# The last group of a fused filter-and-MLP kernel: turned by TensorE, stored in two transfers, with the bound on |h| behind the first layer

## The chip, the cores and the metric

One Trainium2 chip, one of its cores. The metric is the device time of one launch in microseconds; the time before is the median of three runs. A profile is one execution; its span is a few microseconds shorter than the launch.

## What is computed

```python
X = np.fft.rfft(x, axis=1)                    # x: 8 x 3008 x 256
Y = X * (filt_r + 1j * filt_i)[None, :, :]
y = np.fft.irfft(Y, n=3008, axis=1).astype(np.float32)
t = y.reshape(8 * 3008, 256)                  # 24064 tokens
h = t @ w_in                                  # w_in: 256 x 2048
g = h - np.tanh(h)
out = (g @ w_out).astype(np.float32)          # w_out: 2048 x 256
```

The transforms are factored as 64 x 47 and done as products. The second part, two layers around `h - tanh(h)`, is most of the work.

## The kernel before

The tokens are cut into 48 groups of up to 512 columns, over five units of one or two batch entries. A group goes through four steps `u` of the hidden layer. Each layer is done as seven products of half-size blocks instead of eight, with sums of blocks on both sides (q = 1 to 7). The main loop is a pipeline over `U = 4 * group + u`: `up(U)` is the first layer, `shrink(U - 1)` the function, `down(U - 2)` the second layer. All three are woven together by the hooks `d, e` (next piece of `down`), `s` (next piece of `shrink`) and `t(k)` (stores, transforms of the next unit, other side work). The order written is the order on each engine. Line numbers such as L622, used below and in the profile, are given as comments.

The function, and the block sums that follow it on GpSimd:

```python
def combine(b, t):
    G.tensor_sub(t[0], b[0][1], b[0][0])        # L462
    G.tensor_sub(t[1], b[1][1], t[0])           # L463
    G.tensor_sub(t[2], b[1][1], b[0][1])        # L464
    G.tensor_sub(t[3], t[1], b[1][0])           # L465
```

```python
# up(U), first layer                             # products: L483
mm(X, 1, True); mm(Y, 2, True); s1 = copied("s1")     # copies on ScalarE: L489
t(0); d(); s()
V.tensor_add(h[:, 0, :, 0:w], Y, s1)            # L499
e(); s(); s(); t(1)
mm(X, 6, False); mm(Z, 5, True); u2 = copied("u2")
d(); s(); e(); t(2)
mm(X, 7, False); u3 = copied("u3")
V.tensor_add(h[:, 3, :, 0:w], Z, u3)            # L513
d(); s(); e(); t(3)
mm(X, 4, False)
V.tensor_copy(h[:, 2, :, 0:w], X)               # L519
s(); d(); e(); t(4)
mm(Z, 3, False)
V.tensor_add(h[:, 1, :, 0:w], Z, u2)            # L525
```

`shrink` has six pieces: for k = 2 and then 0, `start(k)` (ScalarE, L539 and L540: y), `square(k)` (VectorE L544: h*y; ScalarE L545), `end(k)` (VectorE L548), and behind the last one `combine`.

The second layer adds into four PSUM banks over the four steps. In the last step the blocks of the output are put together:

```python
mm(1, 2)                                        # products: L590
yield
if done:                                        # done = (u == 3)
    ACT.copy(p1, product(1))                    # L603
    V.tensor_add(o[:, 0, 0:w], product(2), p1)  # L604
yield
mm(3, 5)
yield
if done:
    ACT.copy(p5, product(5))                    # L609
    V.tensor_add(x12, product(3), p5)           # L610
yield
mm(6, 7)
yield
if done:
    V.tensor_add(u2, product(6), p1)            # L615
    V.tensor_add(p1, product(7), u2)            # L616
yield
mm(4)
yield
if done:
    V.tensor_add(o[:, 1, 0:w], product(4), p1)  # L621
    G.tensor_add(o[:, 0, w:2 * w], u2, x12)     # L622
    G.tensor_add(o[:, 1, w:2 * w], p1, p5)      # L623
    accs.pop(i)
    stores.append((i, o))
yield
```

`o` has the features in the partitions and the tokens along the rows; the output in memory is the other way round. `store`, called at `t(2)` of the next step, turns it in blocks of 32 x 32 and prepares 32 transfers with rows of 32 floats; four of them are issued at every `t(k)`:

```python
def store(i, o):
    ot = dn.tile([128, 2, CH * 128], F32, tag="ot", bufs=1, name="ot")
    for h in range(2):
        V.transpose(ot[:, h, 0:total], o[:, h, 0:total])     # L637
    # ... blocks: four quarters of the partitions, with their first rows in memory
    for h in range(2):
        for k in range(4):
            for row, m, lo in blocks:
                outs.append((dram(...), ot[32 * k:32 * k + 32, h, :]...))

def store_some(n):
    for dst, src in outs[:n]:
        nc.sync.dma_start(dst, src)                          # L655
    del outs[:n]
```

The function is done by a form that holds for small |h| alone. `bounded` multiplies |w_in| with the largest |t| of each group, which bounds |h|, and counts whether all lie below `NEAR`; behind everything each engine loads the count, and only if it isn't full is the general path run (it isn't run with these inputs).

```python
def bounded(z):
    # ...
    for half in range(2):
        pb = z("pb", [128, NP, ng])                          # ng = 48 groups
        for t in range(NP):                                  # NP = 8
            w_abs = tr.tile([128, 2, 128], F32, tag="x", bufs=3, name="w_abs")
            cols = slice(t * 128, (t + 1) * 128)
            if half == 0:
                ACT.activation(w_abs, wu[:, 0:2, cols], AF.Abs)                 # L671
            else:
                V.tensor_add(w_abs[:, 0], wu[:, 4, cols], wu[:, 3, cols])       # L673
                ACT.activation(w_abs[:, 0], w_abs[:, 0], AF.Abs)                # L674
                ACT.activation(w_abs[:, 1], wu[:, 3, cols], AF.Abs)             # L675
            for h in range(2):
                nc.tensor.matmul(pb[:, t], w_abs[:, h], largest[:, h], ...)     # L677
        V.tensor_single_scalar(out=small[:, half], in_=pb, scalar=NEAR, op=ALU.is_lt)  # L679
        yield
    V.tensor_reduce(out=least, in_=small, axis=mybir.AxisListType.XYZ, op=ALU.min)     # L682
    nc.tensor.matmul(pc, least, ones, start=True, stop=True)                    # L684
    V.tensor_copy(count, pc)                                                    # L685
    yield
```

It is called in `t(k)` of the main loop, three times in the first step of the last group:

```python
if i == len(groups) - 1 and k in (0, 2, 4):
    next(bounds, None)
```

and the end of the kernel is

```python
for w in stores:
    store(*w)
store_some(len(outs))
# ...
within = nc.values_load(count[0:1, 0:1], min_val=0, max_val=128)    # L1060, on every engine
with tc.If(within < 128):                                           # L1061
    ...
```

Of the kernel before, what the change touches and what calls it, by code (L numbers as in the profile page):

```python
# [66 lines left out]
def _consts():  # L67
    wq = np.exp(-2j * np.pi * np.outer(np.arange(NQ), np.arange(NQ)) / NQ)
    wr = np.exp(-2j * np.pi * np.outer(np.arange(NR), np.arange(NR)) / NR)
    tw = np.exp(-2j * np.pi * np.outer(np.arange(NQ), np.arange(NR)) / SEQ)  # L70


    f1 = np.zeros((NQ, 64))
    f1[:, 0:31] = wq.real[:, 1:32]
    f1[:, 31] = wq.real[:, 0]
    f1[:, 32:63] = wq.imag[:, 1:32]
    f1[:, 63] = wq.real[:, 32]

    wf1 = np.zeros((2, 128, 64, 2))
    for b in range(2):  # L80
        wf1[0, 64 * b:64 * b + 64, :, b] = f1
        wf1[1].reshape(128, 2, 64)[64 * b:64 * b + 64, b] = f1
    wf1 = wf1.reshape(2, 128, 128).transpose(1, 0, 2)

    perm = np.arange(NR)
    perm[LO:] = LO + NR - 1 - perm[LO:]
    f2 = np.zeros((NK, R2, R2))
    for a in range(31):  # L90
        wp = (wr * tw[a + 1][None, :])[perm, :]
        f2[a, 0::2] = np.concatenate([wp.real.T, wp.imag.T], axis=1)
        f2[a, 1::2] = np.concatenate([-wp.imag.T, wp.real.T], axis=1)
    f2[:, :, NR + LO:] *= -1.0
    w0, w32 = wr * tw[0][None, :], wr * tw[32][None, :]
    f2[31, 0::2, 0:LO] = w0.real.T[:, 0:LO]
    f2[31, 0::2, NR + 1:NR + LO] = w0.imag.T[:, 1:LO]
    f2[31, 1::2, LO:NR] = w32.real.T[:, 0:HI]
    f2[31, 1::2, NR + LO:R2] = w32.imag.T[:, 0:HI]
    f2[31, 1::2, NR] = w32.real.T[:, HI]  # L100


    f2w = np.zeros((NK, R2, 128))
    f2w[:, :, 0:NR], f2w[:, :, IM:IM + NR] = f2[:, :, :NR], f2[:, :, NR:]


    ctw = np.exp(2j * np.pi * np.outer(np.arange(33), np.arange(NR)) / SEQ)
    g = np.zeros((NK, IM + NR, R2))
    for a in range(31):
        t1 = (wr.conj() * ctw[a + 1][:, None]) / SEQ  # L110
        tr, ti = t1.real.T[perm, :], t1.imag.T[perm, :]
        g[a, :NR, :NR], g[a, :NR, NR:] = tr, ti
        g[a, IM:, :NR], g[a, IM:, NR:] = -ti, tr
    g[:, IM + LO:] *= -1.0
    t0 = (wr.conj() * ctw[0][:, None] / SEQ).T
    t32 = (wr.conj() * ctw[32][:, None] / SEQ).T
    g[31, 0, :NR] = t0.real[0]
    g[31, IM, NR:] = t32.real[HI]
    g[31, 1:LO, :NR], g[31, IM + 1:IM + LO, :NR] = 2 * t0.real[1:LO], -2 * t0.imag[1:LO]
    g[31, LO:NR, NR:], g[31, IM + LO:, NR:] = 2 * t32.real[0:HI], -2 * t32.imag[0:HI]  # L120


    w = np.exp(2j * np.pi * np.outer(np.arange(NQ), np.arange(33)) / NQ)
    s = np.zeros((64, NQ))
    s[0:62:2] = 2.0 * w.real[:, 1:32].T
    s[1:62:2] = -2.0 * w.imag[:, 1:32].T
    s[62] = w.real[:, 0]
    s[63] = w.real[:, 32]
    s2 = np.zeros((128, 128))
    for b in range(2):  # L130
        s2[64 * b:64 * b + 64, 64 * b:64 * b + 64] = s


    fg = np.zeros((IM + RP, NK, 128 + RP2))
    fg[:R2, :, :128] = f2w.transpose(1, 0, 2)
    fg[:IM + NR, :, 128:].reshape(IM + NR, NK, 2, RP)[..., :NR] = \
        g.transpose(1, 0, 2).reshape(IM + NR, NK, 2, NR)

    return [np.ascontiguousarray(v, dtype=np.float32) for v in (wf1, fg.reshape(IM + RP, -1), s2)]


@with_exitstack
def kernel(
# [8 lines left out]
):  # L152
    nc = tc.nc
    V, G, ACT = nc.vector, nc.gpsimd, nc.scalar
    wf1_d, fg_d, s2_d = (
        nc.inline_tensor(v, name=n).ap() for v, n in zip(_consts(), ("wf1", "fg", "s2")))


    ct1 = [nc.dram_tensor(f"ct1_{p}", (RP, 64 * len(bs), DM), F32, kind="Internal")
# [298 lines left out]
        uts[i] = (b, tu, w)  # L458
        yield

    def combine(b, t):
        G.tensor_sub(t[0], b[0][1], b[0][0])  # L462
        G.tensor_sub(t[1], b[1][1], t[0])  # L463
        G.tensor_sub(t[2], b[1][1], b[0][1])  # L464
        G.tensor_sub(t[3], t[1], b[1][0])  # L465


# [59 lines left out]
    def shrink(U):  # L527

        h, w = hs.pop(U)
        ht = {k: h[:, k:k + 2].rearrange("p a b n -> p (a b) n")[:, :, 0:w] for k in (0, 2)}  # L530

        def tiles(tag, bufs):
            return dn.tile([128, 4, 256], F32, tag=tag, bufs=bufs, name=tag)[:, :, 0:w]

        y, sq = {}, {}

        def start(k):
            y[k] = tiles("y", 2)
            ACT.activation(y[k], ht[k], AF.Arctan, scale=S)  # L539
            ACT.activation(y[k], y[k], AF.Square)  # L540

        def square(k):
            sq[k] = tiles("sq", 1)
            V.tensor_mul(ht[k], ht[k], y[k])  # L544
            ACT.activation(sq[k], y[k], AF.Square, bias=near_b, scale=A)  # L545

        def end(k):
            V.scalar_tensor_tensor(out=ht[k], in0=sq[k], scalar=K, in1=ht[k],  # L548
                                   op0=ALU.add, op1=ALU.mult)

        start(2)
        yield
        square(2)
        yield
        end(2)
        yield
        start(0)
        yield
        square(0)
        yield  # L560
        end(0)
        t = dn.tile([128, 4, 2, 256], F32, tag="t", bufs=2, name="t")
        blocks = [[h[:, 2 * a + k, :, 0:w] for k in range(2)] for a in range(2)]
        combine(blocks, [t[:, k, :, 0:w] for k in range(4)])
        gs[U] = (blocks, t, w)
        yield

# [2 lines left out]
    def down(U):  # L570
# [12 lines left out]
        def product(q):  # L583
            bank, k = at[q]
            return acc[bank][:, k, 0:w]
# [28 lines left out]
        if done:  # L614
            V.tensor_add(u2, product(6), p1)  # L615
            V.tensor_add(p1, product(7), u2)  # L616
        yield
        mm(4)
        yield
        if done:  # L620
            V.tensor_add(o[:, 1, 0:w], product(4), p1)  # L621
            G.tensor_add(o[:, 0, w:2 * w], u2, x12)  # L622
            G.tensor_add(o[:, 1, w:2 * w], p1, p5)  # L623
            accs.pop(i)
            stores.append((i, o))
        yield

    def store(i, o):
# [15 lines left out]
# [3 lines that stand above are left out]
# [3 lines left out]
                        ot[32 * k:32 * k + 32, h, :].rearrange(  # L650
                            "p (j c) -> p j c", c=128)[:, 0:m, lo:lo + 32]))

    def store_some(n):
        for dst, src in outs[:n]:
            nc.sync.dma_start(dst, src)  # L655
        del outs[:n]

    def bounded(z):


        ng = len(groups)
        small = tr.tile([128, 2, NP, ng], F32, tag="a2", bufs=2, name="small")
        ones = cst.tile([128, 1], F32, name="ones")
        G.memset(ones, 1.0)
        for half in range(2):
            pb = z("pb", [128, NP, ng])
            for t in range(NP):
                w_abs = tr.tile([128, 2, 128], F32, tag="x", bufs=3, name="w_abs")
                cols = slice(t * 128, (t + 1) * 128)
                if half == 0:  # L670
                    ACT.activation(w_abs, wu[:, 0:2, cols], AF.Abs)  # L671
                else:
                    V.tensor_add(w_abs[:, 0], wu[:, 4, cols], wu[:, 3, cols])  # L673
                    ACT.activation(w_abs[:, 0], w_abs[:, 0], AF.Abs)  # L674
                    ACT.activation(w_abs[:, 1], wu[:, 3, cols], AF.Abs)  # L675
                for h in range(2):
                    nc.tensor.matmul(pb[:, t], w_abs[:, h], largest[:, h],  # L677
                                     start=(h == 0), stop=(h == 1), skip_group_check=True)
            V.tensor_single_scalar(out=small[:, half], in_=pb, scalar=NEAR, op=ALU.is_lt)  # L679
            yield  # L680
        least = cst.tile([128, 1], F32, name="least")
        V.tensor_reduce(out=least, in_=small, axis=mybir.AxisListType.XYZ, op=ALU.min)  # L682
        pc = z("pc", [1, 1])
# [3 lines that stand above are left out]
# [69 lines left out]
    with tc.tile_pool(name="tr", bufs=2) as tr:  # L756
# [184 lines left out]
        with tc.tile_pool(name="dn", bufs=2) as dn, \  # L941
                tc.tile_pool(name="ps", bufs=1, space=bass.MemoryType.PSUM) as ps:

            psums.append(lambda name, shape: ps.tile(shape, F32, tag="t", bufs=1, name=name))

            def tiles1(k, dtype, n):

                tag = {"raw": "ft", "it": "uv", "pt": "zs", "st": "e1", "ft": "a2"}[k]
# [24 lines left out]
            with tc.manual_schedule():  # L973
# [3 lines left out]
                for U in range(total + 2):  # L977
# [39 lines left out]
                    def t(k):  # L1017
# [11 lines left out]
                        elif done < len(steps) and steps[done] <= pos:  # L1029
# [5 lines left out]
                            if done == n_f:  # L1035
                                ms = middle(p + 1, z1)
                                next(ms)
                        if i == len(groups) - 1 and k in (0, 2, 4):
                            next(bounds, None)
                        if k in (0, 2, 4):  # L1040
                            next(late, None)
                        elif U > 0:
# [2 lines left out]
                    if U < total:  # L1045
                        if i == len(groups) - 1 and u == 0:
                            bounds = bounded(z1)
                        up(U, d, e, s, t)
                    else:
                        for k in range(5):  # L1050
# [2 lines left out]
                            d()  # L1053
                            e()
                            t(k)
                for w in stores:
                    store(*w)
                store_some(len(outs))
# [36 lines left out]
```

## Time and profile before

| | before |
|---|---|
| time, median of 3 (lowest to highest) | 2882.33 us (2880.47 to 2883.72) |
| span of the profiled run | 2879.3 us |
| busy: TensorE products, VectorE, ScalarE, GpSimd | 95%, 69%, 65%, 61% |
| mean granted clock of TensorE | 0.984 |
| transfers of L655 | 1536 |
| products of the bound, L677 | 64 instructions, from 2787.1 to 2799.9 us |
| last output turned (L637); last transfer issued | 2858.2 us; 2873.8 us |

PE is TensorE, PEld its loads of weights, DVE is VectorE, ACT ScalarE, POOL GpSimd, SP SyncE. A q behind the name means the engine's sequencer or its queue. A product of fp32 operands is shown as two instructions. In a line on waits, the numbers are microseconds in total, how often, and the longest. Matmul ends are modelled, so idle time of PE in such lines is a lower limit.

### The profile page before, as it was taken

The page shows a single profiled execution, that of the slowest core. Times are in us where ns is not written, and L with a number is a line of the kernel's source. Part 1 is how long each engine was busy: PE and PEld are TensorE (multiplying, and loading weights), DVE is VectorE, ACT ScalarE, POOL GpSimd, SP SyncE. Part 2 cuts the span into 40 slices and gives each one's busy share as a digit, 9 for nine tenths or more (in the row PEclk, how much of TensorE's full clock was granted, in tenths as well). Part 3 has the DMA queues.
Part 4 walks back from the last instruction along what each step waited for, and adds up shares of the span by engine and source line. Part 5 has one row for each costly group of instructions (what it writes and reads, how often), then busy time and mean ns, then how long its engine had stood idle before and what let it go on. Part 6 is the DMA issues. An engine that isn't in the chain of part 4 may idle for free.

```text
span 2879.3 us, 36469 instructions
## 1 busy us (share of the span) xinstructions
PE 2748.1 (95%) x12474; PEld 2278.9 (79%) x12474; DVE 1989.3 (69%) x2214; ACT 1872.2 (65%) x2460; POOL 1743.4 (61%) x1382
## 2 busy tenths in 40 slices
PE   5789999999999999999999999999999999999996
PEld 3467777888878787888877888888888888888885
DVE  4675666766776677766677777766777777777765
ACT  3555666666767676666666676666666676666663
POOL 4345777544677767645576777655476666555544
PEclk7889999999999999999999999999999999999998
DMA  9644443232233332222323233112233222110100
GB/s 270 180 150 116 114 110 91 62 93 81 70 76 84 76 75 53 57 81 83 87 71 75 68 78 81 36 45 67 51 75 81 53 55 56 24 28 16 26 11 16
DMA packets 328061, 217.46 MB, mean 76 GB/s; under 512 B 229085, under 2 KB 280405, under 8 KB 327674
## 3 DMA queue, kind: packets, MB, share of 16 engines
q1 hardware_dynamic: 273176, 160.50, 23.6%
q10 hardware_dynamic: 52738, 51.33, 5.9%
q0 software_dynamic: 1952, 3.22, 0.5%
q8 instruction: 100, 1.64, 0.2%
q14 instruction: 95, 0.78, 0.1%
HBM read 138.81 MB, written 79.17 MB: 76 GB/s over the span
## 4 chain that ended last, share of the span: by engine, by line
PE 69%; DVE 9%; ACT 8%; POOL 5%; issue 4%; DMA 3%; SPq 1%; ACTq 0%; DVEq 0%; POOLq 0%
PE o L590 27%; PE x L483 18%; PE z L483 8%; PE y L483 5%; PE pe L364 3%; PE pu L447 3%; DVE h L544 3%; PE pz L383 3%; ACT y L539 2%; PE pf L304 2%; ACT y L540 1%; POOL t L465 1%; ACT u L489 1%; DVE uv L398 1%; DVE h L519 1%
## 5 line engine op out<-in xcount | busy, mean ns | idle before, releaser
L590 PE MATMUL o<-t,wd 128*128 128x256 f32 (+2 forms) x3072 | 777.9, 376 | 1.8 <-POOL t L464 1.3
L544 DVE TENSOR_TENSOR h<-h,y 128x1024 f32<-128x1024 f32 (+2 forms) x384 | 589.7, 1536 | 256.1 <-ACT y L540 255.9
L462 POOL TENSOR_TENSOR t<-h 128x512 f32<-128x512 f32 (+2 forms) x192 | 240.1, 1250 | 767.5 <-DVE h L548 582.3
L590 PEld LDWEIGHTS o<-t,wd 128*128 128x128 f32 x3072 | 582.0, 191 | 74.4 <-POOL t L464 1.9
L483 PE MATMUL x<-tu,wu 128*128 128x256 f32 (+2 forms) x2304 | 592.2, 380 | 16.5 <-ACT u L489 15.5
L590 PE MATMUL o<-h,wd 128*128 128x256 f32 (+2 forms) x2304 | 581.6, 375 | 0.2 <-DVE h L548 0.2
L548 DVE SCALAR_TENSOR_TENSOR h<-sq,h 128x1024 f32<-128x1024 f32 (+2 forms) x384 | 566.6, 1476 | 20.8 <-ACT y L539 0.5
L483 PEld LDWEIGHTS x<-tu,wu 128*128 128x128 f32 x2304 | 430.2, 191 | 157.2 <-issue 73.2
L590 PEld LDWEIGHTS o<-h,wd 128*128 128x128 f32 x2304 | 431.3, 190 | 70.8 <-issue 18.5
L545 ACT ACTIVATE sq<-y,near_b 128x1024 f32<-128x1024 f32 (+2 forms) x384 | 435.4, 1134 | 5.8 <-DVE h L548 1.1
L539 ACT ACTIVATE y<-h 128x1024 f32<-128x1024 f32 (+2 forms) x384 | 400.0, 1042 | 14.8 <-ACT e L367 6.8
L489 ACT COPY s<-x 128x512 f32<-128x512 f32 (+2 forms) x192 | 110.7, 577 | 458.2 <-PE x L483 449.6
L540 ACT ACTIVATE y<-y 128x1024 f32<-128x1024 f32 (+2 forms) x384 | 399.3, 1040 | 12.2
L465 POOL TENSOR_TENSOR t<-t,h 128x512 f32<-128x512 f32 (+2 forms) x192 | 306.7, 1597 | 0.0
L489 ACT COPY u<-x 128x512 f32<-128x512 f32 (+2 forms) x384 | 219.2, 571 | 73.0 <-PE x L483 35.5
L399 POOL TENSOR_TENSOR zs<-zs,ft 128x512 f32<-128x512 f32 x112 | 166.3, 1485 | 142.3 <-ACT zs L397 142.2
L463 POOL TENSOR_TENSOR t<-h,t 128x512 f32<-128x512 f32 (+2 forms) x192 | 241.6, 1258 | 15.0
L464 POOL TENSOR_TENSOR t<-h 128x512 f32<-128x512 f32 (+2 forms) x192 | 249.5, 1300 | 0.0
L400 POOL TENSOR_TENSOR uv<-uv,zs 128x512 f32<-128x512 f32 x112 | 211.3, 1887 | 16.0 <-DVE uv L398 7.8
L483 PE MATMUL x<-ut,wu 128*128 128x256 f32 (+2 forms) x768 | 200.0, 383 | 12.2 <-DVE h L519 10.7
L483 PE MATMUL z<-tu,wu 128*128 128x256 f32 (+2 forms) x768 | 195.4, 377 | 0.5 <-DVE h L525 0.5
L483 PE MATMUL z<-ut,wu 128*128 128x256 f32 (+2 forms) x768 | 194.8, 376 | 0.0
(113 smaller groups left out, 3236.6 us busy)
## 6 DMA issues: line engine op xcount, KB each, us to landing
a<-ct SPq DMA_DIRECT2D x64, 384.0 KB
ct<-e ACTq DMA_DIRECT2D x128, 192.0 KB
ft<-filt SPq DMA_DIRECT2D x96, 256.0 KB
out_dram<-ot SPq DMA_DIRECT2D x1408, 16.0 KB
ct<-a ACTq DMA_DIRECT2D x80, 256.0 KB
x_sb<-in_x_dram SPq DMA_DIRECT2D x69, 256.0 KB
e<-ct SPq DMA_DIRECT2D x33, 512.0 KB
fg<-fg SPq DMA_DIRECT2D x40, 392.0 KB
```

The lines of the kernel that those rows point to most:

```text
L462: G.tensor_sub(t[0], b[0][1], b[0][0])
L463: G.tensor_sub(t[1], b[1][1], t[0])
L464: G.tensor_sub(t[2], b[1][1], b[0][1])
L465: G.tensor_sub(t[3], t[1], b[1][0])
L483: nc.tensor.matmul(bank[:, k], wu[:, q - 1, (2 * u + k) * 128:(2 * u + k + 1) * 128], rhs[q - 1], start=(first and k == 0), stop=True, ski ...
L489: ACT.copy(t, X)
L539: ACT.activation(y[k], ht[k], AF.Arctan, scale=S)
L540: ACT.activation(y[k], y[k], AF.Square)
L544: V.tensor_mul(ht[k], ht[k], y[k])
L545: ACT.activation(sq[k], y[k], AF.Square, bias=near_b, scale=A)
L548: V.scalar_tensor_tensor(out=ht[k], in0=sq[k], scalar=K, in1=ht[k], op0=ALU.add, op1=ALU.mult)
L590: nc.tensor.matmul(product(q), wd[:, q - 1, (2 * u + k) * 128: (2 * u + k + 1) * 128], rhs[q - 1][:, k], start=(u == 0 and k == 0 and q == ...
```

## The change

Four edits. (1) The second of the four output blocks (L622) is added by GpSimd as soon as its inputs are there, one piece earlier; this holds for every group. (2) The products of the bound leave the first step of the last group: |w| is made ready in eight pieces in the first two steps of the last group and kept, the products of the first half come in the drain behind the last step of the first layer, and those of the second half, with the minimum and the count, behind the last output. (3) The last group is turned by TensorE (a product with the identity), copied out of PSUM by ScalarE and VectorE, and stored in two transfers with rows of up to 4 KB, one from SyncE and one from ScalarE. (4) In the very last step one of the four block sums goes to VectorE. It is meant to shorten what follows the last product and to free the first step of the last group.

```diff
+    (the identity, np.eye(128), is one more constant "one"; it is loaded in the first step
+     of the last group)

-    def combine(b, t):
+    def combine(b, t, shared=False):
         G.tensor_sub(t[0], b[0][1], b[0][0])
         G.tensor_sub(t[1], b[1][1], t[0])
-        G.tensor_sub(t[2], b[1][1], b[0][1])
+        (V if shared else G).tensor_sub(t[2], b[1][1], b[0][1])
         G.tensor_sub(t[3], t[1], b[1][0])
 ...
-        combine(blocks, [t[:, k, :, 0:w] for k in range(4)])
+        combine(blocks, [t[:, k, :, 0:w] for k in range(4)], U + 1 == 4 * len(groups))
 ...
             V.tensor_add(u2, product(6), p1)
             V.tensor_add(p1, product(7), u2)
+            G.tensor_add(o[:, 0, w:2 * w], u2, x12)
         yield
         mm(4)
         yield
         if done:
             V.tensor_add(o[:, 1, 0:w], product(4), p1)
-            G.tensor_add(o[:, 0, w:2 * w], u2, x12)
             G.tensor_add(o[:, 1, w:2 * w], p1, p5)
             accs.pop(i)
-            stores.append((i, o))
+            if i + 1 < len(groups):
+                stores.append((i, o))
+            else:
+                store_last(i, o)
 ...
+    def store_last(i, o):
+        p, c = groups[i]
+        r, n = CHUNKS[p][c]
+        ws_ = widths(p, c)
+        full = ws_.count(128)
+        ot = dn.tile([128, CH, DM], F32, tag="ot", bufs=1, name="ot")
+        for h, copy in ((0, ACT.copy), (1, V.tensor_copy)):
+            pt = psl([128, CH, 128], "xy"[h])
+            for j, w in enumerate(ws_):
+                nc.tensor.transpose(pt[0:w, j], o[:, h, j * 128:j * 128 + w], one)
+            cols = slice(h * 128, (h + 1) * 128)
+            copy(ot[:, 0:full, cols], pt[:, 0:full])
+            if full < n:
+                copy(ot[0:64, full:n, cols], pt[0:64, full:n])
+        ...  # two batch entries: one transfer; one entry, as here:
+            for h, rows, r_h, n_h in halves(p, r, n):
+                (nc.sync, ACT)[h].dma_start(
+                    dram(out.tensor, (b * SEQ + r_h) * DM, [[NR * DM, 64], [1, n_h * DM]]),
+                    ot[rows, 0:n_h])
 ...
     def bounded(z):
+        w_abs = [tr.tile([128, 2, DFF // 2], F32, tag="ft", bufs=2, name="w_abs")
+                 for _ in range(2)]
+        for half in range(2):
+            for t in range(4):
+                cols = slice(t * 256, (t + 1) * 256)
+                if half == 0:
+                    ACT.activation(w_abs[0][:, :, cols], wu[:, 0:2, cols], AF.Abs)
+                else:
+                    V.tensor_add(w_abs[1][:, 0, cols], wu[:, 4, cols], wu[:, 3, cols])
+                    ACT.activation(w_abs[1][:, 0, cols], w_abs[1][:, 0, cols], AF.Abs)
+                    ACT.activation(w_abs[1][:, 1, cols], wu[:, 3, cols], AF.Abs)
+                yield
         for half in range(2):
             pb = z("pb", [128, NP, ng])
             for t in range(NP):
-                (|w| of 128 columns made here)
                 for h in range(2):
-                    nc.tensor.matmul(pb[:, t], w_abs[:, h], largest[:, h], ...)
+                    nc.tensor.matmul(pb[:, t], w_abs[half][:, h, t * 128:(t + 1) * 128],
+                                     largest[:, h], ...)
+                if t == NP // 2 - 1 and half == 0:
+                    yield
             V.tensor_single_scalar(out=small[:, half], in_=pb, scalar=NEAR, op=ALU.is_lt)
-            yield
+            if half == 0:
+                yield
 ...
-                        if i == len(groups) - 1 and k in (0, 2, 4):
-                            next(bounds, None)
+                        if i == len(groups) - 1 and U + 2 < total and k != 1:
+                            next(bounds)
 ...
                             e()
                             t(k)
+                            if U == total and k in (1, 2):
+                                next(bounds)
+                next(bounds)
                 for w in stores:
                     store(*w)
```

More of the change, by code (lines that the diff above doesn't have):

```diff
@@ L137, in _consts @@
         g.transpose(1, 0, 2).reshape(IM + NR, NK, 2, NR)
-    return [np.ascontiguousarray(v, dtype=np.float32) for v in (wf1, fg.reshape(IM + RP, -1), s2)]
+    return [np.ascontiguousarray(v, dtype=np.float32)
+            for v in (wf1, fg.reshape(IM + RP, -1), s2, np.eye(128))]
 @with_exitstack
@@ L154 @@
     V, G, ACT = nc.vector, nc.gpsimd, nc.scalar
-    wf1_d, fg_d, s2_d = (
-        nc.inline_tensor(v, name=n).ap() for v, n in zip(_consts(), ("wf1", "fg", "s2")))
+    wf1_d, fg_d, s2_d, one_d = (
+        nc.inline_tensor(v, name=n).ap() for v, n in zip(_consts(), ("wf1", "fg", "s2", "one")))
     ct1 = [nc.dram_tensor(f"ct1_{p}", (RP, 64 * len(bs), DM), F32, kind="Internal")
@@ L651, in store @@
                             "p (j c) -> p j c", c=128)[:, 0:m, lo:lo + 32]))
+    def store_last(i, o):
[12 more added lines that the diff above has]
+                copy(ot[0:64, full:n, cols], pt[0:64, full:n])
+        b = UNITS[p][0]
+        if len(UNITS[p]) == 2:
+            nc.sync.dma_start(dram(out.tensor, (b * SEQ + r) * DM, [[NR * DM, 128], [1, n * DM]]),
+                              ot[:, 0:n])
+        else:
[3 more added lines that the diff above has]
+                    ot[rows, 0:n_h])
     def store_some(n):
@@ L664, in bounded @@
         G.memset(ones, 1.0)
+        w_abs = [tr.tile([128, 2, DFF // 2], F32, tag="ft", bufs=2, name="w_abs")
[5 more added lines that the diff above has]
+                    ACT.activation(w_abs[0][:, :, cols], wu[:, 0:2, cols], AF.Abs)
+                else:
+                    V.tensor_add(w_abs[1][:, 0, cols], wu[:, 4, cols], wu[:, 3, cols])
+                    ACT.activation(w_abs[1][:, 0, cols], w_abs[1][:, 0, cols], AF.Abs)
+                    ACT.activation(w_abs[1][:, 1, cols], wu[:, 3, cols], AF.Abs)
+                yield
         for half in range(2):
@@ L667, in bounded @@
             for t in range(NP):
[L668 to L675, printed above, removed]
-                for h in range(2):
-                    nc.tensor.matmul(pb[:, t], w_abs[:, h], largest[:, h],
-                                     start=(h == 0), stop=(h == 1), skip_group_check=True)
+                for h in range(2):
+                    nc.tensor.matmul(pb[:, t], w_abs[half][:, h, t * 128:(t + 1) * 128],
+                                     largest[:, h], start=(h == 0), stop=(h == 1),
+                                     skip_group_check=True)
+                if t == NP // 2 - 1 and half == 0:
+                    yield
             V.tensor_single_scalar(out=small[:, half], in_=pb, scalar=NEAR, op=ALU.is_lt)
-            yield
+            if half == 0:
+                yield
         least = cst.tile([128, 1], F32, name="least")
@@ L944, with psl @@
             psums.append(lambda name, shape: ps.tile(shape, F32, tag="t", bufs=1, name=name))
+            def psl(shape, tag):
+                return ps.tile(shape, F32, tag=tag, bufs=1, name="pt")
             def tiles1(k, dtype, n):
@@ L1047 @@
                             bounds = bounded(z1)
+                            one = tr.tile([128, 128], F32, tag="x", bufs=3, name="one_sb")
+                            nc.sync.dma_start(one, one_d)
                         up(U, d, e, s, t)
```

## The prediction

> **What bounds the kernel now.** I read the page first (busy shares, clock row), then who waits for whom on TensorE, then the chain of work that ended last around one group boundary, around the last group and at the end, and last the busy times by stretch.
>
> ```profile
> PE 2748.1 (95%) x12474; PEld 2278.9 (79%) x12474; DVE 1989.3 (69%) x2214; ACT 1872.2 (65%) x2460; POOL 1743.4 (61%) x1382
> ```
>
> TensorE is busy for 95% of the span: the kernel is a stream of products, and a change can win only where TensorE stands still, where it does work that can go elsewhere, and after its last product. There are three such places.
>
> First, the boundary between groups. From the answers on waits (TensorE's, then VectorE's from 200 to 2780 us) and the chain that ended last:
>
> ```profile
> PE x L483 <- DVE h L519: 10.7, 26, 0.9
> ...
> DVE ot L637 <- POOL o L622: 18.1, 28, 1.8
> ```
>
> ```profile
> 2661.59 2.21 POOL t L465
> 2663.80 1.68 POOL o L622
> 2665.51 1.41 DVE ot L637 x2
> 2667.49 1.13 DVE h L544
> 2669.27 1.13 PE x L483 x4
> ```
>
> A chain line is start, length, engine, tile, line. GpSimd adds the last sums of a group (L622) only after the four sums of the next unit (L462 to L465), though the input of L622 is ready long before (8 us earlier in the group before the last: L615 at 2818.5, L622 at 2826.4). VectorE waits for L622 before its two transposes (L637), and the copy L519 behind them holds TensorE. The 26 waits sum to 10.7 us, but the modelled ends of matmuls hide a part: the last three such periods are 50.7 us long, while 224 instructions of products at 0.216 us (chain pieces of 0.86 for four) and 16 of L447 at 0.111 (0.89 for eight) make 50.1. So a wait written as about 0.3 us is really near 0.57.
>
> Second, the first unit of the last group. Busy by stretch; the columns are the stretch, its length, then PE, PEld, DVE, ACT, POOL busy (instructions), clock, DMA share, GB/s:
>
> ```profile
> 2774.50:2786.04 11.54, 11.54 (x59) 10.20 (x58) 8.56 (x8) 7.55 (x9) 6.26 (x7) 1.00 0.19 29
> 2786.04:2809.69 23.65, 21.14 (x123) 19.04 (x122) 11.38 (x21) 14.34 (x33) 7.25 (x8) 0.93 0.00 1
> 2809.69:2821.03 11.34, 11.34 (x57) 10.62 (x57) 7.70 (x13) 7.60 (x11) 2.49 (x4) 1.00 0.00 0
> ```
>
> and the chain in the middle one:
>
> ```profile
> 2787.14 3.77 PE pb L677 x32
> ...
> 2796.33 4.02 PE pb L677 x32
> ...
> 2806.94 0.87 DVE least L682
> ```
>
> The unit with the bound takes 23.65 us; its neighbours take 11.3 to 11.5. Excess: 12.2 us. Of it 7.8 are products of the bound; the rest is waiting for |w| from ScalarE, for the minimum on VectorE, and a clock of 0.50 between 2800 and 2802 us, where four products took 1.83 instead of 0.92 us.
>
> Third, the end:
>
> ```profile
> 2849.66 5.95 PE o L590 x28
> ...
> 2856.98 0.66 DVE ot L637
> ```
>
> ```profile
> 2857.66 16.57 SPq L655 DMA_DIRECT2D out_dram<-ot  x32
> ```
>
> The last product ends near 2856.4 us, the second transpose at 2858.2, and then SyncE issues 32 stores, one per 0.5 us. The span ends at 2879.3: 5.1 us behind the last issue. TensorE's own branch at the end took 3.6 us, VectorE's semaphore came 2.9 us after its branch, SyncE's 2.7, and the closing exchange of semaphores lasts 2.3 us (2877.0 to 2879.3).
>
> **What the Trainium skill says.** "VectorE: DVE Perf Modes", section "The three transpose paths": VectorE turns only 32x32 blocks, TensorE a whole 128x128 into PSUM, from where it must be copied. This agrees with the kernel: because of the blocks it stores 128-byte pieces, 4096 packets under 512 B in the last 25 us. "GPSIMD Engine Reference", section "Specifications": GpSimd shares its way into SBUF with VectorE, in contention when VectorE has two SBUF inputs. The trace agrees: L622 takes 1.70 us beside VectorE's L548, 0.66 at the quiet end (224 columns); L548 itself 2.1 instead of 1.2. "TensorE: Matmul & The Clock Gate", section "What's actually happening": the clock is halved after an idle window of some 3.4 us; here it falls to 0.50 behind the 48-column products. "DMA: Bandwidth & Descriptors", section on measured bandwidth: 64 KB at 138 GB/s, 1 MB at 341 GB/s (loads; no trace here has such a large store by itself). My estimate from that page for 448 KB in two stores is 1.4 to 3.3 us.
>
> **Part 1, L622 earlier (every group).** Its add is now given to GpSimd directly behind the two VectorE sums that feed it, before the four sums of the next unit. GpSimd is idle there (7.5 us before L462 in these groups), so nothing is delayed. Behind L465 remains only L623. It takes over the contended time of L622 (1.7 us, 2663.8 to 2665.5), but the first transpose no longer waits: it can start when VectorE ends L548 at 2664.9, and the second follows at 2665.6, when L623 is done. VectorE gains 0.56 to 0.62 us, about as much as TensorE's true wait of 0.57. If all 26 waits go: 26 x 0.5 = 13 us. Groups with transforms in between have more waits of other kinds, so I count 11 us.
>
> **Part 2, the bound out of the unit.** Removed: the 12.2 us of excess. Added in the first two units of the last group: eight pieces of |w|. A piece of 512 elements costs ScalarE about 0.6 us (L540: 1.04 for 1024; L489: 0.57 for 512), two of 256 cost 0.8 with an add of about 0.4 on VectorE (L673: 0.29 for 128). That is 2.4 us on ScalarE in one unit and 3.2 + 1.7 (VectorE) in the next; ScalarE has 3.7 us free per unit. Most lies beside TensorE, but a piece stands directly ahead of the copy u3 (L489), which VectorE awaits, and VectorE is nearly full in the second unit (9.34 of 11.32 in the following one). I charge 2 us. Net: -10.
>
> **Part 3, the end.** In the drain the first half of the products comes in two bursts of 16 instructions, 1.9 us each (3.77/2). TensorE was waiting 1.8 us there for GpSimd's sums (1.3 for L464, 0.5 for L465), so of 3.8 us about 2 are new, less what VectorE's help with the very last L464 gives (0.2): the last product ends 1.2 to 2 us later, near 2858 on the old axis, more if the clock falls. Then:
> - o complete 0.7 us later; eight transposes like L447's products (eight instructions 0.89, two per product): 1.8 us, the first four beside the wait for L623: o + 1.5, thus 2860.2.
> - copy of the second half, 384 and 128 columns on VectorE: 0.55 + 0.3: 2861.1. Stores issued 2861.5. The loads of 64 to 72 KB that the page lists with a time land 2.8 to 3.3 us after their issue; with 1 us more for the size by the estimate above, landed at about 2865.5.
> - beside the copies: second half of the products, 32 instructions, 4.0 us: 2864.2; L679 0.56 + L682 0.95: 2865.8; the one product and the cast with their waits 0.7: 2866.5; value load 0.5: 2867.0; branch 3.6 on TensorE: 2870.6; closing exchange 2.3: 2872.9.
>
> So I expect the count, not the stores, to end last. 2879.3 - 2872.9 = 6.4 us won; for a halved clock in the 48-column products I take off 1.4: -5.
>
> Sum: -11 - 10 - 5 = -26. From 2882.3: about 2856 us.
>
> **The rivals.**
> (a) The count takes the place of the stores completely. The second-half products stand behind everything, at a clock of 0.50 (8 us instead of 4, as the fall at 2800 us suggests), and all engines must load the count before they branch. Before, it was ready at 2808.3 and cost nothing at the end. Then part 3 wins 0 to 1 us: total near 2861.
> (b) The group waits don't come from L622. Once VectorE is freed, L623 or ScalarE's y (VectorE waits 249.8 us for it in all) may end last. For: L623 runs into the same contention. Against: it is needed only by the second transpose. Part 1 wins 0 to 4: total near 2866.
> (c) Each wait falls fully, smaller unlisted ones with it, and |w| hides fully: parts 1 and 2 win 17 and 12, total near 2847.
> (d) The stores alone: if one believes only the 16.6 us of issue, the end falls by some 12 us and the count is hidden. Against it: the sum above has five dependent steps behind the last transpose.
>
> **Range and chances.** Part 1 lies between 2 and 17, part 2 between 7 and 12, part 3 between 0 and 9. They are independent; added by squares about +-12. Range 2844 to 2868. Two per cent is 57.6 us, twice the whole sum: faster by more than that 0.02, within 0.97, slower 0.01.
>
> **What would show it.** Right: the waits of TensorE on L519 nearly gone, periods of late groups near 50.1 us instead of 50.7, VectorE's wait at L637 for L622 gone; the first unit of the last group at 11.5 to 13 us; two stores at the end, and the chain ending in pb, least, count. Wrong: the same wait under L623 or y; the clock at 0.50 in the last 25 us over the products; the two stores ending last; or units of the last group that are longer than 13 us because ScalarE is late.

## The result, and the profile after

| | before | changed |
|---|---|---|
| time, median of 5 (lowest to highest) | 2882.08 us (2880.47 to 2883.72) | 2852.54 us (2849.59 to 2855.64) |
| span of the profiled run | 2879.3 us | 2850.8 us |

The ratio is 0.9901, 95% interval 0.9888 to 0.9915: 29.5 us less, which is under 2%. 2856 us was predicted, with a range of 2844 to 2868.

One line was added above the functions shown, so L483, L519 or L590 of before are now L484, L520 and L591; the early add is L618, the last add on GpSimd L624, VectorE's transposes L641.

**Where the 28.5 us between the two profiles lie.** The start of each step of the first layer, read from the traces, cuts the span into four parts:

| part of the span | before | after | difference | predicted |
|---|---|---|---|---|
| start to the fourth group | 337.1 | 333.9 | -3.2 | 0 |
| fourth group to the last (44 groups) | 2448.2 | 2439.7 | -8.5 | -11 |
| first three steps of the last group | 46.2 | 37.4 | -8.8 | -10 |
| last step to the end | 47.8 | 39.7 | -8.1 | -5 |

The first row can't be put down to the change, though edit (1) acts in the first three groups too: in the four profiles of kernels that don't differ up to the fourth group (before and three of the runs below) it starts anywhere from 329.0 to 337.1 us. What the traces show of the change is the other three rows, 25.4 us.

**The boundary between groups.** The page's first line, and two lines on waits (TensorE's; VectorE's from 200 to 2770 us):

```profile
PE 2744.0 (96%) x12482; PEld 2276.7 (80%) x12482; DVE 1983.7 (70%) x2211; ACT 1871.5 (66%) x2450; POOL 1738.0 (61%) x1381
```

```profile
PE x L484 <- DVE h L520: 6.5, 13, 1.0
...
DVE ot L641 <- POOL o L624: 3.7, 3, 1.2
```

Half of the 26 waits on that copy are gone, and VectorE hardly waits at the transposes any more (3 times with 3.7 us instead of 28 with 18.1). One late boundary in order of time (start, length, engine, line):

```profile
2645.49 0.72 POOL L618 TENSOR_TENSOR o<-pu,x 128x256 f32<-128x256 f32 x1 [5.29 <-DVE pu L616]
...
2651.56 2.27 POOL L466 TENSOR_TENSOR t<-t,h 128x512 f32<-128x512 f32 x1
2653.79 1.71 POOL L624 TENSOR_TENSOR o<-p,p 128x256 f32<-128x256 f32 x1
...
2654.84 1.42 DVE L641 STREAM_TRANSPOSE ot<-o 128x512 f32<-128x512 f32 x2
```

The early add finds GpSimd idle and takes 0.72 us. Its old place, and its old length of 1.7 us beside VectorE's L549, are now taken by L624, but the first transpose starts at 2654.84, the moment VectorE ends L549, and L624 ends at 2655.5, before the second one needs it.

**The last group.** Busy time in its first three steps, from y product to y product, columns as in the prediction's table:

```profile
2774.41:2785.75 11.34, 11.34 (x58) 10.62 (x57) 7.60 (x9) 9.67 (x13) 5.73 (x5) 1.00 0.00 0
2785.75:2800.22 14.47, 12.14 (x57) 10.37 (x56) 10.20 (x15) 9.54 (x17) 5.79 (x5) 1.00 0.00 0
2800.22:2811.82 11.60, 11.13 (x58) 10.37 (x58) 9.61 (x14) 7.57 (x11) 6.06 (x5) 1.00 0.06 10
```

The first step is down from 23.65 to 11.34 us: TensorE busy to the last tenth, with four pieces of |w| beside it. The second step has become 3.1 us longer (11.34 before). In the middle of it the chain of work that ended last runs like this:

```profile
2794.19 0.34 DVE w_abs L702
...
2794.55 0.42 ACT w_abs L703
2794.97 0.31 ACT w_abs L704
2795.27 0.43 ACT u L490
```

VectorE adds two blocks of the weights (L702), ScalarE stands and waits for that sum, and the copy that TensorE needs (L490) stands behind it in ScalarE's queue. Four such waits of ScalarE take 6.3 us in all. Later in the same step a third sum (2798.06, 0.71 us) stands in VectorE's own queue, directly ahead of the copy L520. TensorE waits for both copies (from the timeline, the wait in brackets):

```profile
2795.74 1.02 PE L484 MATMUL x<-tu,wu 128*128 128x224 f32 x4 [1.30 <-ACT u L490]
...
2799.36 1.02 PE L484 MATMUL x<-ut,wu 128*128 128x224 f32 x4 [0.97 <-DVE h L520]
```

**The end**, the chain that ended last:

```profile
2830.33 5.38 PE o L591 x28
...
2836.92 1.16 PE pt L667 x7
2838.08 3.52 PE pb L710 x32
...
2841.62 0.57 DVE small L715
...
2842.22 0.96 DVE least L719
...
2843.54 0.15 DVE count L722
```

The chain of work ends in the count. The two stores are issued 4.6 us before it is there, and TensorE's branch comes behind the load of the count (2843.7, 0.5 us):

```profile
2838.76 0.52 ACTq L678 DMA_DIRECT2D out_dram<-ot  x1
2838.93 0.51 SPq L678 DMA_DIRECT2D out_dram<-ot  x1
```

```profile
L1106 PEldq COMPARE_BRANCH  x1: 3852/3852/3852, 2844.3 to 2844.3; - x1
```

The DMA engines are done with the stores at about 2841.8 us (share of 0.97 from 2840 to 2841 us, 0.68 in the next microsecond, then 0): hidden behind the count.

### The profile page after: what moved, and what is told of

Read it like the earlier page. It is cut to its first block, busy times and chain, and to the rows that moved or that the text cites. A ratio compares the mean times of both kernels' runs of the same rounds, so it can differ in the third digit from the quotient of the medians.

```text
span 2850.8 us, 36441 instructions
## 1 busy us (share of the span) xinstructions
PE 2744.0 (96%) x12482; PEld 2276.7 (80%) x12482; DVE 1983.7 (70%) x2211; ACT 1871.5 (66%) x2450; POOL 1738.0 (61%) x1381
## 4 chain that ended last, share of the span: by engine, by line
PE 77%; ACT 8%; DVE 6%; issue 3%; DMA 3%; POOL 1%; SPq 1%; ACTq 1%; DVEq 0%; POOLq 0%
PE o L591 31%; PE x L484 20%; PE z L484 9%; PE y L484 5%; PE pe L365 3%; PE pu L448 3%; PE pz L384 3%; ACT y L540 2%; PE pf L305 2%; DVE h L545 2%; ACT y L541 1%; DVE uv L399 1%; ACT zs L398 1%; ACT u L490 1%; DMA filt<-in_filt_i_dram 1%
## 5 line engine op out<-in xcount | busy, mean ns | idle before, releaser
L591 PE MATMUL o<-t,wd 128*128 128x256 f32 (+2 forms) x3072 | 775.8, 375 | 0.0
L545 DVE TENSOR_TENSOR h<-h,y 128x1024 f32<-128x1024 f32 (+2 forms) x384 | 582.1, 1516 | 258.1 <-ACT y L541 258.1
L591 PEld LDWEIGHTS o<-t,wd 128*128 128x128 f32 x3072 | 580.6, 190 | 71.7
L484 PE MATMUL x<-tu,wu 128*128 128x256 f32 (+2 forms) x2304 | 591.6, 379 | 18.4 <-ACT u L490 16.9
L549 DVE SCALAR_TENSOR_TENSOR h<-sq,h 128x1024 f32<-128x1024 f32 (+2 forms) x384 | 569.9, 1484 | 20.8 <-ACT y L540 0.5
L591 PE MATMUL o<-h,wd 128*128 128x256 f32 (+2 forms) x2304 | 581.1, 375 | 0.2 <-DVE h L549 0.2
L484 PEld LDWEIGHTS x<-tu,wu 128*128 128x128 f32 x2304 | 429.4, 191 | 161.5 <-issue 73.3
L591 PEld LDWEIGHTS o<-h,wd 128*128 128x128 f32 x2304 | 430.9, 190 | 70.9 <-issue 19.1
L490 ACT COPY s<-x 128x512 f32<-128x512 f32 (+2 forms) x192 | 110.8, 577 | 439.8 <-PE x L484 431.2
L490 ACT COPY u<-x 128x512 f32<-128x512 f32 (+2 forms) x384 | 219.4, 571 | 68.6 <-PE x L484 33.3
L484 PE MATMUL x<-ut,wu 128*128 128x256 f32 (+2 forms) x768 | 198.8, 381 | 8.1 <-DVE h L520 6.5
L500 DVE TENSOR_TENSOR h<-y,s 128x512 f32<-128x512 f32 (+2 forms) x192 | 130.2, 678 | 96.2 <-PE y L484 86.0
L484 PE MATMUL z<-tu,wu 128*128 128x256 f32 (+2 forms) x768 | 194.5, 376 | 0.1
```

The source lines that it names most:

```text
L484: nc.tensor.matmul(bank[:, k], wu[:, q - 1, (2 * u + k) * 128:(2 * u + k + 1) * 128], rhs[q - 1], start=(first and k == 0), stop=True, ski ...
L490: ACT.copy(t, X)
L591: nc.tensor.matmul(product(q), wd[:, q - 1, (2 * u + k) * 128: (2 * u + k + 1) * 128], rhs[q - 1][:, k], start=(u == 0 and k == 0 and q == ...
```

## The experiments

Three questions were open: how much of the gain comes from the early add, why the second step of the last group grew, and what ends last at the end. Beside each run the kernel before was run again on the same chip. Line numbers in its profile are those of its own program.

**The early add alone.**

```diff
             V.tensor_add(p1, product(7), u2)
+            G.tensor_add(o[:, 0, w:2 * w], u2, x12)
 ...
-            G.tensor_add(o[:, 0, w:2 * w], u2, x12)
             G.tensor_add(o[:, 1, w:2 * w], p1, p5)
```

> The kernel before with edit (1) alone: L622 directly behind L616 in every group. Theory A: only the waits of TensorE at the first product of the fourth step (behind the two transposes) come from L622; these gaps fall from about 8.5 us to about 2 us in all and the periods of groups 43 to 46 from 50.7 to 50.1 us; about 8.5 us of the whole gain, 2873.5 us. Rival B, as the prediction had it: all 26 waits on the copy L519 come from it, 11 to 13 us, 2869 to 2871 us. Rival C: the gain seen before the sixth group (3.2 us) is chance of that one profile and the rest smaller, 5 us, 2877 us.

Measured: 2871.5 us against 2879.9, ratio 0.9969 (0.9960 to 0.9978). The time lies between theory A (2873.5) and rival B (2869 to 2871); the trace decides. From the fourth group to the last it is 8.6 us shorter, as in the changed kernel. The periods of groups 43 to 46 fall from 50.7 to 50.13 us (51.4 to 50.8 in the last). The waits:

```profile
PE x L483 <- DVE h L519: 5.5, 12, 0.6
```

The 26 listed waits of before fall into two kinds: 14 (5.3 us) stand ahead of the first product of the fourth step, the one behind the transposes, and 12 (5.4 us) ahead of the first products of the other three. In this run 1 (0.5 us) and 11 (5.0 us) are left. The same with all gaps, taken as the distance of two starts less the usual 0.216 us: up to the last group there are 21 with 8.5 us ahead of the fourth step before and 7 with 2.0 us here; at the other steps nothing changes (27 with 10.7 us, 27 with 10.4). Theory A holds: L622 was behind those waits alone. B is out, and so is C, for the stretch wins 8.6 us and not 5.

**The bound alone**, with the old add, VectorE's transposes and 32 transfers in the last group (edits (1), (3) and (4) taken back; one cut of it, against the changed kernel):

```diff
-            if i + 1 < len(groups):
-                stores.append((i, o))
-            else:
-                store_last(i, o)
+            stores.append((i, o))
```

> The kernel before with edit (2) alone: the bound moved, the last group still turned by VectorE and stored in 32 transfers. In this program SyncE loads the count ahead of the last 32 transfers. Theory A: the first two steps of the last group win 8.8 us, but the late count now holds back the transfers: count loaded some 21.7 us after the start of the drain, then 16.6 us of issue, 3.9 of branch and 2.3 of closing, 45 us from the start of the drain instead of 36.8; net -0.5 us, 2881.5 us. Rival: the count hides beside the transfers as it did before, and the whole of 8.8 us less 1.5 for the products in the drain remains, about 2875 us.

Measured: 2878.4 us against 2879.9, ratio 0.9992 (0.9983 to 1.0000). The first three steps of the last group win 9.1 us, and from the last step to the end it takes 54.3 us instead of 47.8. From the timeline (VectorE's transposes are L638 here, the stores L681):

```profile
2853.29 0.15 DVE L719 CAST count<-pc 1x1 int32<-1x1 f32 x1 [0.37 <-PE pc L718]
2853.69 1.17 DVE L638 STREAM_TRANSPOSE ot<-o 128x448 f32<-128x448 f32 x2 [0.25 <-issue]
2854.40 17.35 SPq L681 DMA_DIRECT2D out_dram<-ot  x32
```

The net result is near what theory A said: the end grew by 6.5 us instead of 8.2. The reason is half of what I wrote: not only SyncE's load of the count, already VectorE's transposes stand behind the whole count in their queue, though the output was there at 2848.9 us. With the old way of storing the moved bound is worth next to nothing.

This run also tells what edit (4) is worth, which was not tried by itself: the last output comes 26.4 us after the start of the last step here without it, and 26.4 us after it in the changed kernel. The 0.2 us that I counted for it don't show.

**The turn by TensorE alone**, with the bound still in the first step of the last group (one cut):

```diff
+            if i + 1 < len(groups):
+                stores.append((i, o))
+            else:
+                store_last(i, o)
```

> The kernel before with edit (3) alone: the last group turned by TensorE and stored in two transfers, the bound still in the first step of the last group. Theory A: with the count ready early, the end is last output 2857.4, eight transposes and copies to 2858.9, issue to 2859.4, branch and fetch 3.9, closing 2.3: 2865.6 instead of 2879.3, that is -13.7 us, about 2868.3 us. Rival: the landing of 448 KB in two transfers takes 5 us or more from its issue and ends last: -10 to -12 us, 2870 to 2872 us.

Measured: 2870.9 us against 2879.9, ratio 0.9973 (0.9962 to 0.9985). From the last step to the end 34.9 us instead of 47.8: -12.9, near the -13.7 of theory A. The two stores are done at 2862.9 us, 3.1 us after the issue of the second and 4.5 us before the end, so they neither take 5 us nor end last, and the rival is out. But the first step of the last group took 30.2 us instead of 23.7. The clock is the number ahead of the last two in the line (busy times by stretch):

```profile
2798.00:2800.00 2.00, 2.00 (x11) 1.97 (x10) 0.59 (x2) 1.01 (x4) 0.00 (x0) 0.50 0.00 0
```

In this form the identity shares three buffers with the |w| of the bound. The same again with a tile of its own:

```diff
-    one = tr.tile([128, 128], F32, tag="x", bufs=3, name="one_sb")
+    one = cst.tile([128, 128], F32, name="one_sb")
```

> Edit (3) alone once more, with the identity in a tile of its own. In the first run of it the first step of the last group took 30.2 us instead of 23.7, while the end won 12.8. Theory A: the identity takes one of the three buffers that the bound's |w| uses in that step, TensorE waits more often and its clock falls for longer; with a tile of its own the step is back at 23.7 us (within 1) and the end keeps 12.8 us: 2867 us. Rival: the step's length is the state of the clock in that one execution; then it can be anything from 22 to 30 us, whatever the tile.

Measured: 2866.3 us against 2880.0, ratio 0.9953 (0.9939 to 0.9967); the end is 34.8 us, the first step of the last group 25.3 us, so theory A's "within 1" of 23.7 is missed by 0.6. The intervals of the two runs overlap, and their traces speak for the rival. The same first 32 products of the bound, behind the same wait, in the first run and in the second:

```profile
2781.53 6.03 PE L706 MATMUL pb<-largest,w_abs 128*128 128x48 f32 x32 [0.18 <-ACT w_abs L700]
...
2786.77 3.77 PE L706 MATMUL pb<-largest,w_abs 128*128 128x48 f32 x32 [0.18 <-ACT w_abs L700]
```

In the first run the clock fell to 0.50 in the middle of them (2784.0), and once more in the second burst of 32. Four profiles have the bound in its old place:

| profile | clock at 0.50 in the step | length of the step | above the shortest |
|---|---|---|---|
| early add alone | 0 us | 22.0 us | 0 |
| before | 3.4 us | 23.7 us | 1.7 us |
| turn, own tile | 6.8 us | 25.3 us | 3.3 us |
| turn, shared buffer | 13.7 us | 30.2 us | 8.2 us |

Half of the time at 0.50 (1.7, 3.4 and 6.8 us) is nearly the whole difference. What the shared buffer adds by itself are two more waits of TensorE for |w|, 0.28 us each, in the second burst. That it brought about the longer fall of the clock isn't shown: the first fall came ahead of these waits.

**GpSimd makes the sum of weights, one step earlier**, in the changed kernel:

```diff
                     ACT.activation(w_abs[0][:, :, cols], wu[:, 0:2, cols], AF.Abs)
+                    G.tensor_add(w_abs[1][:, 0, cols], wu[:, 4, cols], wu[:, 3, cols])
                 else:
-                    V.tensor_add(w_abs[1][:, 0, cols], wu[:, 4, cols], wu[:, 3, cols])
```

> The changed kernel, but the sum of two weight blocks that the second half of |w| needs is made by GpSimd in the first step of the last group instead of by VectorE directly ahead of ScalarE in the second. Theory A: the second step takes 14.4 us instead of 11.3 because ScalarE, in order, stands and waits for VectorE's sum (6.3 us of waits) and holds its copies; with the sum ready it takes 11.3 to 12 us: -2.5 to -3 us, about 2849.5 us. Rival: it is ScalarE's own 0.82 us per piece that lengthens the step, or GpSimd's sum slows VectorE in the first step by as much: no change, 2852 us.

```profile
2776.42:2787.78 11.36, 11.36 (x58) 10.54 (x57) 7.64 (x8) 9.68 (x13) 8.75 (x8) 1.00 0.00 0
2787.78:2799.61 11.83, 11.60 (x57) 10.53 (x57) 9.23 (x13) 9.84 (x19) 8.15 (x6) 1.00 0.00 0
2799.61:2810.49 10.88, 10.86 (x57) 10.52 (x57) 9.75 (x13) 7.07 (x9) 6.87 (x5) 1.00 0.07 11
```

The second step is back at 11.8 us and the third at 10.9, with the first still at 11.4; ScalarE does the same 0.82 us per piece as before. So the rivals are out, and the cause is shown: the sum on VectorE, not ScalarE's own work. The run takes away both of its effects at once, ScalarE's wait for it and its place ahead of VectorE's own copy L520, so it doesn't tell how much each costs. The three steps together are 3.4 us shorter, and 3.5 us in the next variant, which has the same sum. In the time of the launch this can't be seen: 2851.5 us against 2879.9, ratio 0.9905 (0.9890 to 0.9920), next to the changed kernel run again:

> The changed kernel again, unaltered, as the measure for the two variants beside it on the same chip. 2850 to 2853 us; in the trace groups 3 to 46 the same to 1 us, the steps of the last group 11.3, 14.4, 11.7 us, last step to end 39.7 us. What varies should lie before the fourth group, where single profiles of kernels with the same code there have differed by up to 8 us.

Measured: 2853.1 us against 2880.0, ratio 0.9906 (0.9890 to 0.9921). The steps of the last group and the end repeat to 0.1 us, and so does the stretch from the fourth group to the last to 0.2. The gain over before is 26.9 us in this run, where it was 29.5. The intervals of the two ratios cover 8 to 9 us, far more than 3.4.

**The count ahead of the last outputs**: with GpSimd's sum, and with the second half of the bound's products ahead of the last step of the second layer.

```diff
         V.tensor_reduce(out=least, in_=small, axis=mybir.AxisListType.XYZ, op=ALU.min)
+        yield
 ...
-                            if U == total and k in (1, 2):
+                            if U == total and k in (1, 2, 3):
```

> As with GpSimd's sum, and the second half of the bound's products ahead of the last step of the second layer as well; only the last product and the cast stay behind the outputs. Theory A: TensorE does the same work, so the last output comes 3.5 us later, but the count is then ready with it; what ends last is issue, load, branch with its fetch (6.2 to 7.1 us from SyncE's branch to the end): last step to end 39 to 40 us, no change of more than 1 us. Rival: the chain from the last transposes to the count (products 3.5, compare, minimum, product, cast 2.1, load 0.5 us) is fully won except for 3.5: -2 to -2.6 us.

Measured: 2852.7 us against 2880.0, ratio 0.9905 (0.9890 to 0.9920); from the last step to the end 40.2 us, 0.5 more than with GpSimd's sum alone. Theory A: counted from the start of the last step, the output came 4.1 us later and the count 0.7 us earlier than in the changed kernel, and SyncE's load of the count, now beside the two stores, took 1.0 us instead of 0.5.

**Without the second half of the products** (left out: the products and the compare of half of the hidden units, which are taken as in bounds):

```diff
-        for half in range(2):
+        G.memset(small[:, 1], 1.0)
+        for half in range(1):
             pb = z("pb", [128, NP, ng])
```

> The changed kernel without the second half of the bound's products and its compare (left out: the half of the units that these cover is taken as in bounds; |w| of it is still made). Theory A: the count ends last in the changed kernel, so leaving 32 instructions (3.5 us) and 0.6 us of compare out moves the end by that less what the two stores then hold back the fetch behind the branch: -2.3 to -3.6 us from last step to end. Rival: the two stores end last already, no change.

Measured: 2850.2 us against 2880.0, ratio 0.9899 (0.9884 to 0.9914); in the trace 36.8 us from the last step to the end instead of 39.7: -2.9, of 4.1 us left out. So the count does end last in the changed kernel, and the rival is out. Of the rest, 0.7 us isn't won because VectorE's minimum now stands behind its copies of the output (the count comes 3.4 us earlier, not 4.1), and 0.6 us is given back behind the count (the load is L1106 in this run):

```profile
L1106 PEldq TENSOR_LOAD <-count x1: 1124/1124/1124, 2840.2 to 2840.2; - x1
```

The load of the count took 1.1 us on every engine, beside the two stores, instead of 0.5.

## Why the prediction was right, and where it was off

**Part 1, the early add (11 us predicted, 8.5 measured).** The mechanism was right down to the contended 1.7 us that L623, now L624, takes over and the 0.57 us per boundary. The step that failed is "If all 26 waits go: 26 x 0.5 = 13 us", cut to 11 without a count: 13 of the 26 waits on that copy are still there. They look alike in the list, since it names the line and not the step of the group; only in the step behind the transposes was L622 the cause. Splitting the gaps by step first would have given 21 with 8.5 us, of which 6.5 went. With the early add alone the third steps, which end at these gaps, are 7.1 us shorter over the 44 groups, the fourth steps 1.6 us, and the first two steps the same to 0.1; where the 1.6 us come from stays open.

**Part 2, the bound out of the unit (10 us predicted, 8.8 measured).** What was taken out was right: 12.3 us (23.65 to 11.34). The term mis-sized is "I charge 2 us": the pieces of |w| cost 3.5 us in all three steps, 3.0 of it in the second, none in the first. I had named the right place, a piece ahead of a copy that others await, and a full VectorE, but counted the wait as ScalarE's own time. It is the order of three engines: VectorE's sum, then ScalarE's |w|, then the copy for TensorE. The sum was also counted too small: about 0.4 us each, while the four took 0.41, 0.71, 1.24 and 1.30 us, the two long ones beside block sums on GpSimd. And 1.7 of the 12.3 us taken out are the fall of the clock in the profile of before; against the early add alone, where it didn't fall, the same edit wins 1.7 us less.

**Part 3, the end (5 us predicted, 8.1 measured).** The chain was right, step by step: count last, stores hidden. Four terms were too large: the last product came 0.5 to 0.6 us later, not 1.2 to 2; eight transposes are one instruction each and not two, so that they were done 0.6 us behind the last output and not 1.5; the 32 products took 3.5 and not 4.0 us; and "for a halved clock in the 48-column products I take off 1.4" was not needed: the clock stayed at 1.00 until TensorE's last product. Against that, the branch and what follows it took 0.6 us more than counted (3.9 and 2.6 us for 3.6 and 2.3). The 2.8 to 3.3 us from issue to landing were the short ones of the profile's list, which also has 4.4 and 7.6 to 7.9 us for 64 KB; the stores were done 2.9 us after the issue of the second, where about 4 had been counted.

**The rivals.** (a) is half right: the count is what ends last, but with the clock at 1.00 it wins 8 us and not 0 to 1. (b) is out for the waits behind the transposes: with L622 gone, 14 of 21 vanish, and the longer time of its successor on GpSimd is awaited only 3 times. (c) is out, for 13 waits stay and |w| doesn't hide. (d) is out: stores alone win 12.9 us at the end, but with the bound moved as well the end wins 8.1. Beside the new stores the moved bound therefore costs 4.9 us at the end (34.8 to 39.7), and in the first three steps it wins 6.5 us over the early add alone (43.9 to 37.4), where the clock stayed up. By this estimate it is worth 1.6 us, and more only where the clock falls at the old place (1.7 us in the profile of before, 3.3 in the turn with its own tile). Old bound, early add and new stores together were not run.

**The sum.** The three parts were -26 and came to -25.4; the rest of the 29.5 us lies before the fourth group, where executions differ anyway, and in the spread of the launches (26.9 us when run again). That the total was hit so closely is partly luck: the errors of parts 1 and 3 cancel. The range was wider than its own working: the three ranges added by squares give +-9 (11 with the longer sides), not +-12. The measured time lies inside either.

## What to carry to other kernels

A list of waits sums over places that only look alike: before a wait is multiplied by its count, ask at which step of the loop it stands and whether the cause that is to be removed is there too. Work for another engine hides only if what stands behind it in that engine's queue isn't awaited; a chain of two engines ahead of a copy costs its wait, not its busy time. An edit can be worth nothing until another is made, as the moved bound was with the old stores. And before two single profiles are compared, look whether the clock fell in one of them: here that made up to 6.8 us of one step.

## What the runs showed of the hardware that was not expected

- The branch at the end takes the engines 2.5 to 4.9 us from its compare to the next instruction (TensorE 3.6 before, 3.9 changed, 4.9 with the count in the drain). In the turn alone, SyncE and ScalarE, which branched while their two stores were moving, came 4.8 and 4.5 us behind it.
- A TensorE transpose of 128x128 in fp32 is one instruction, 0.11 to 0.17 us apart, while a product of the same size is two at 0.11 each.
- Where the 64 products of the bound stood as two bursts of 32 in the middle of the layers, the clock fell to 0.50 for 3.4, 6.8 and 13.7 us in three profiles, and not at all in a fourth with the same bursts and nearly the same waits (early add alone). With the moved bound (bursts of 16, 16 and 32) it stayed at 1.00 in all six profiles, but for the last 0.1 us of these products in one. What decides isn't shown.
- 448 KB in two transfers, rows of 4 KB and 3 KB, moved within 1.9 us (2839.9 to 2841.8), and were done 2.9 us after the issue of the second.
